# A GELU feed-forward kernel on one Trainium2 core: two opening loads move from SyncE's DMA queue to ScalarE's

## The chip, the cores and the metric

The kernel runs on one core of one Trainium2 chip. The metric is device time in microseconds (us), the median of several runs. One more execution was taken with the hardware profiler; all rows below are from that one. Its times are counted from the first instruction.

## What is computed

Two dense layers with a tanh-approximated GELU between them, all tensors in bf16:

```python
B, S, D, F = 1, 2048, 448, 1792
# x: (B, S, D)   w1: (D, F)   b1: (F)   w2: (F, D)   b2: (D)
h = einsum("bsd,df->bsf", x, w1) + b1
h = gelu(h, approximate=True)
out = einsum("bsf,fd->bsd", h, w2) + b2
```

## The kernel before

**Tiling.** The 2048 rows of x are cut into four chunks of 512 (`SC`), the 1792 hidden columns into 14 tiles of 128 (`ft`). D = 448 isn't a multiple of 128, so it is held in four slots whose first rows are `KROW = [0, 128, 256, 320]`; slots 2 and 3 overlap by 64 rows, and each hidden tile is summed from three full slots and one half (lines 229 and 237). The first layer writes PSUM with the hidden column on the partitions, ScalarE applies GELU with b1 as its bias and writes `g_sb` (L340), the second layer multiplies `g_sb` with w2 (L317), and VectorE adds b2 (L358). SyncE stores the result.

**Order.** `schedule` runs seven blocks of eight hidden tiles and the second layer's chunks between them, in an order written out by hand. There is no planner: each engine has its own program, and semaphores join them.

**The opening.** x for chunk 0 is loaded in rows, not transposed, into `xn_sb` (four row groups of 128 rows each, 512 rows in all). It comes in two halves of 224 KB: groups 0 and 1 on `sem_xn[0]` (L172), groups 2 and 3 on `sem_xn[1]` (L173). TensorE transposes it by matmuls with an identity (L214), in the six parts of `XPARTS`; VectorE and ScalarE copy the parts in turn from PSUM to `xT_sb` (L352 and L336). The first two parts need the first half of x, the third and all later ones the second half too. Ahead of the third part stands a small matmul that turns b1 (L205).

`opening_block` (L247) then runs block 0, eight hidden tiles with one PSUM bank each, slot by slot:

- slot 0 of w1 for the eight tiles. Its columns 0 to 1023 come in two pieces of 512 columns, 128 KB each (`W0_PIECES`, L146): tile 0 waits for piece 0 on `sem_w10[0]`, tile 4 for piece 1 on `sem_w10[1]`. Tile 0 also waits until VectorE has copied the first slot's two parts (`sem_xTd` at 2, L257); the other tiles wait for the copies that free their banks;
- slot 1 for the eight tiles, behind `sem_w1[1]` (L265);
- slots 2 and 3, behind `sem_w1[2]` and `sem_w1[3]` (L268, L269), then the halves.

Block 1 begins behind `sem_w1r` (L312), the remaining columns of w1. From there on no load is near: w2 is first used when the second layer's chunk 0 runs.

**The loads.** SyncE issues, in this order: the two halves of x (L172, L173), the two pieces of w1's slot 0 (L146), slots 1, 2 and 3 up to column 1024 (L150, 256 KB each), the rest of w1 (L151, L154), the transposing loads of x's chunk 1 (L164), w2 (L158), b2 (L178) and the transposing loads of chunks 2 and 3. ScalarE issues b1 (L330, 3.5 KB), then loads its activation table and runs a throwaway activation (L332), then copies its three parts of x (L336). The profile names SyncE's queue of data packets q1 and ScalarE's q10.

```python
sp.dma_start(xn_sb[:, 0:2, :], x0_view[:, 0:2, :]).then_inc(sem_xn[0], 16)
sp.dma_start(xn_sb[:, 2:4, :], x0_view[:, 2:4, :]).then_inc(sem_xn[1], 16)
load_w1(sp)
load_xT(sp, 1)
```

Of the kernel before, what the change touches and what calls it, by code (L numbers as in the profile page):

```python
# [11 lines left out]
def bass_standalone__dense_activation_gelu__prompt_kernel(  # L12
# [10 lines left out]
    P = 128  # L23
# [15 lines left out]
    W0_PIECES = [(0, 4), (4, 8)]  # L39
# [45 lines left out]
    for what, c in schedule:  # L85
        if what == "l1":
            jobs += [("g", order.index(tile)) for part in BLOCKS[c] for tile in part]
        else:
            jobs += [("o", n) for n, (j, _, _) in enumerate(outs) if j // STC == c]
    number = {job: n for n, job in enumerate(jobs)}  # L90

    with ExitStack() as es:
        sb = lambda n, s, d: es.enter_context(nc.sbuf_tensor(n, s, d))
        xT_sb = sb("xT_sb", [P, NKT, S], BF16)
        w1_sb = sb("wi_sb", [P, NKT, F], BF16)
        w2_sb = sb("wo_sb", [P, NFT, D], BF16)
        xn_sb = sb("xn_sb", [P, STC, D], BF16)
# [10 lines left out]
        sem_w10 = [S_(f"sem_w10_{i}") for i in range(len(W0_PIECES))]  # L108
# [4 lines left out]
        sem_xn = [S_(f"sem_xn{i}") for i in range(2)]  # L113
# [17 lines left out]
        x0_view = x2[0:SC, :].rearrange("(p t) d -> p t d", t=STC)  # L131
        out0_view = out2[0:SC, :].rearrange("(p t) d -> p t d", t=STC)

        def out_dram(j):
            return out0_view[:, j, :] if j < STC else out2[j * P:(j + 1) * P, :]

        def x_part(n, parts):
            h, k = parts[0]
            to = xT_sb[:, k:k + len(parts), 2 * h * P:2 * (h + 1) * P]
            src = ps[XBANK + n][:, 0:2 * P * len(parts)]  # L140
            return to, src.rearrange("p (k t) -> p k t", k=len(parts))

        def load_w1(eng):
            with nc.allow_non_contiguous_dma(reason="w1 column pieces"):
                for i, (a, b) in enumerate(W0_PIECES):
                    eng.dma_start(  # L146
                        w1_sb[:, 0, a * P:b * P], w1[0:P, a * P:b * P]
                    ).then_inc(sem_w10[i], 16)
                for k, r in list(enumerate(KROW))[1:]:
                    eng.dma_start(w1_sb[:, k, 0:WCUT], w1[r:r + P, 0:WCUT]).then_inc(sem_w1[k], 16)  # L150
                eng.dma_start(  # L151
                    w1_sb[:, 0:3, WCUT:F], w1[0:3 * P, WCUT:F].rearrange("(k p) f -> p k f", p=P)
                ).then_inc(sem_w1r, 16)
                eng.dma_start(w1_sb[:, 3, WCUT:F], w1[KROW[3]:D, WCUT:F]).then_inc(sem_w1r, 16)  # L154

        def load_w2(eng, i):
            a, b = W2_PIECES[i]
            eng.dma_start(  # L158
                w2_sb[:, a:b, :], w2[a * P:b * P, :].rearrange("(ft p) d -> p ft d", p=P)
            ).then_inc(sem_w2[i], 16)  # L160

        def load_xT(eng, c):
            for k, d0 in enumerate(KROW):
                eng.dma_start(  # L164
                    xT_sb[:, k, c * SC:(c + 1) * SC],
                    x2[c * SC:(c + 1) * SC, d0:d0 + P],
                    transpose=True,
                ).then_inc(sem_x[c], 16)

        @block.sync  # L170
        def _(sp):
            sp.dma_start(xn_sb[:, 0:2, :], x0_view[:, 0:2, :]).then_inc(sem_xn[0], 16)  # L172
            sp.dma_start(xn_sb[:, 2:4, :], x0_view[:, 2:4, :]).then_inc(sem_xn[1], 16)  # L173
            load_w1(sp)
            load_xT(sp, 1)
            for i in range(len(W2_PIECES)):
                load_w2(sp, i)
            sp.dma_start(b2_bc[:, :], b2.partition_broadcast(P)).then_inc(sem_b2, 16)  # L178
            for c in range(2, NSC):
                load_xT(sp, c)  # L180
            for j in range(NST - 1):
                sp.wait_ge(sem_osb, j + 1)
                sp.dma_start(out_dram(j), out_sb[:, j, :]).then_inc(sem_od, 16)
            sp.wait_ge(sem_od, 16 * NST)
# [11 lines left out]
        def _(pe):  # L196
# [5 lines left out]
            for n, (_, parts) in enumerate(XPARTS):  # L202
                if n == 2:
                    pe.wait_ge(sem_b1n, 16)
                    pe.matmul(  # L205
                        ps[NB - 1][:, 0:NFT], lhsT=b1n_sb[:, :], rhs=ident[0:NFT, 0:NFT],
                        start=True, stop=True,
                    ).then_inc(sem_b1T, 1)
                for h, k in parts:
                    if (h, k) in ((0, 0), (1, 0)):  # L210
                        pe.wait_ge(sem_xn[h], 16)
                    for t in range(2):
                        col = parts.index((h, k)) * 2 * P + t * P
                        mm = pe.matmul(  # L214
                            ps[XBANK + n][:, col:col + P],
                            lhsT=xn_sb[:, 2 * h + t, KROW[k]:KROW[k] + P],
                            rhs=ident[:, :],
                            start=True, stop=True,
                        )
                mm.then_inc(sem_xtp, 1)  # L220
# [25 lines left out]

            def opening_block(first, second):  # L247
                first = [ft for _, ft in first]
                second = [ft for _, ft in second]

# [77 lines left out]
        @block.scalar  # L328
        def _(act):
            act.dma_start(b1n_sb[:, :], b1.rearrange("(c p) -> c p", p=P)).then_inc(sem_b1n, 16)  # L330
            zero = nc.const_aps.tensor(0.0, [P, 8], FP32)
            act.activation(act_junk[:, :], zero, ACT.Gelu_apprx_tanh)  # L332
            for n, (e, parts) in enumerate(XPARTS):
                if e == "a":
                    act.wait_ge(sem_xtp, n + 1)
                    act.copy(*x_part(n, parts)).then_inc(sem_xTa, 1)  # L336
            act.wait_ge(sem_b1, 1)
            for i, (c, ft) in enumerate(order):
                act.wait_ge(sem_l1, i + 1)
                act.activation(  # L340
                    g_sb[:, ft, c * SC:(c + 1) * SC], bank("g", i)[:, :], ACT.Gelu_apprx_tanh,
                    bias=b1_f[:, ft:ft + 1], scale=1.0,
                ).then_inc(sem_g, 1)
            act.wait_ge(sem_osb, len(outs))
            act.dma_start(out_dram(NST - 1), out_sb[:, NST - 1, :]).then_inc(sem_od, 16)
# [44 lines left out]
```

## Time and profile before

| | us |
|---|---|
| median of 3 runs (lowest to highest) | 96.71 (96.46 to 96.75) |
| the profiled execution | 96.25 |
| its span, from the first to the last instruction | 94.4 |
| around the span in that execution | 1.85 |
| TensorE matmuls busy (granted clock 1.0 throughout) | 90.5 |
| ScalarE busy | 35.9 |
| VectorE busy | 11.7 |
| data moved, mean over the span | 7.50 MB, 79 GB/s |

A row of the timeline gives the start and the length in us, the engine, the line, the operation, what it writes and reads, how many instructions the row merges, and in brackets the idle time before it with what ended it. PE is TensorE's matmul side, PEld its weight loads, SPq and ACTq the sequencers of SyncE and ScalarE as they issue DMAs. The length of an issue isn't that of its transfer: from the start of an issue to the last of the sixteen semaphore increments of its transfer (its landing) it took

| load, line | issue starts | issue to landing | lands |
|---|---|---|---|
| x, first half, L172 | 0.74 | 2.5 | 3.2 |
| x, second half, L173 | 1.19 | 2.7 | 3.9 |
| w1 slot 0, piece 0, L146 | 1.65 | 3.5 | 5.1 |
| w1 slot 0, piece 1, L146 | 2.12 | 3.4 | 5.5 |
| w1 slot 1, L150 | 2.60 | 4.6 | 7.2 |
| w1 slot 2, L150 | 3.07 | 4.8 | 7.9 |
| w1 slot 3, L150 | 3.55 | 5.0 | 8.6 |

### The profile page before, as it was taken

How to read it: one execution, taken by the hardware profiler on the slowest of the kernel's cores; microseconds unless marked ns; L12 is line 12 of the kernel's file. 1: busy time of each engine (PE TensorE's matmuls, PEld its weight loads, DVE VectorE, ACT ScalarE, POOL GpSimd, SP SyncE). 2: the span in 40 equal slices, each digit the busy share in tenths (PEclk: the TensorE clock that was granted, in tenths of full speed). 3: DMA queues.
4: the chain of work that ended last, by engine and by line, in shares of the span. 5: the costliest groups of instructions: out<-in, count | busy, mean ns of one | idle time of the engine just before them, and what ended most of it. 6: DMA issues, size and time to landing. Idle time of an engine off the chain costs nothing.

```text
span 94.4 us, 1159 instructions
## 1 busy us (share of the span) xinstructions
PE 90.5 (96%) x492; PEld 43.8 (46%) x492; DVE 11.7 (12%) x21; ACT 35.9 (38%) x61; POOL 0.7 (1%) x6
## 2 busy tenths in 40 slices
PE   6989999999999999999999999999999999999990
PEld 4724343443443555544344455554345555555670
DVE  0320000000000022220000001222000222222130
ACT  3520595985958910000793990000099000000000
POOL 2000000000000000000000000000000000000000
PEclk9999999999999999999999999999999999999999
DMA  1999999998520010011000001110000110011111
GB/s 36 275 312 280 192 225 350 301 74 166 111 56 0 0 49 28 27 49 49 3 0 0 0 0 49 49 53 24 28 0 0 49 48 16 33 49 56 49 49 49
DMA packets 12385, 7.50 MB, mean 79 GB/s; under 512 B 7004, under 2 KB 11996, under 8 KB 12380
## 3 DMA queue, kind: packets, MB, share of 16 engines
q1 hardware_dynamic: 12208, 7.31, 32.9%
q10 hardware_dynamic: 172, 0.12, 0.4%
q8 instruction: 4, 0.07, 0.3%
q14 instruction: 1, 0.01, 0.0%
HBM read 4.02 MB, written 1.84 MB: 62 GB/s over the span
## 4 chain that ended last, share of the span: by engine, by line
PE 90%; DMA 5%; SPq 2%; DVE 0%; issue 0%
PE ps L317 45%; PE ps L229 38%; PE ps L237 7%; DMA wi_sb<-in_w_dram 5%; SPq L146 1%; SPq L173 0%; SPq L172 0%; DVE out_sb L358 0%
## 5 line engine op out<-in xcount | busy, mean ns | idle before, releaser
L340 ACT ACTIVATE g_sb<-ps,bi_f 128x512 bf16<-128x512 f32 x56 | 33.1, 702 | 34.9 <-PE ps L237 34.9
L317 PE MATMUL ps<-wo_sb,g_sb 128*128 128x448 bf16 (+2 forms) x238 | 42.9, 341 | 0.0
L229 PE MATMUL ps<-xT_sb,wi_sb 128*128 128x512 bf16 x168 | 38.2, 380 | 0.6 <-DMA wi_sb<-in_w_dram 0.4
L317 PEld LDWEIGHTS ps<-wo_sb,g_sb 128*128 128x128 bf16 x238 | 23.1, 98 | 19.7
L229 PEld LDWEIGHTS ps<-xT_sb,wi_sb 128*128 128x128 bf16 x168 | 15.7, 98 | 21.8 <-issue 3.0
L358 DVE TENSOR_TENSOR out_sb<-ps,bo_bc 128x448 bf16<-128x448 f32 (+2 forms) x17 | 10.2, 597 | 76.8 <-PE ps L317 76.8
L237 PE MATMUL ps<-xT_sb,wi_sb 64*128 64x512 bf16 x56 | 7.3, 379 | 0.0
L237 PEld LDWEIGHTS ps<-xT_sb,wi_sb 64*128 64x128 bf16 x56 | 2.2, 94 | 4.6 <-issue 3.0
L200 PE MATMUL ps<-const-bfloat16-1.0 128*128 128x256 bf16 x13 | 2.9, 410 | 0.8 <-PEq L375 0.8
L200 PEld LDWEIGHTS ps<-const-bfloat16-1.0 128*128 128x128 bf16 x13 | 1.8, 140 | 1.5 <-issue 0.7
L352 DVE CAST xT_sb<-ps 128x256 bf16<-128x256 f32 (+1 forms) x3 | 1.4, 510 | 3.8 <-PE ps L214 3.8
L332 ACT ACT_TABLE_LOAD x1 | 1.3, 1283 | 1.4 <-PEq L375 1.4
L336 ACT CAST xT_sb<-ps 128x256 bf16<-128x256 f32 (+1 forms) x3 | 1.3, 443 | 1.1 <-PE ps L214 1.0
L214 PE MATMUL ps<-ident,xn_sb 128*128 128x128 bf16 x16 | 1.2, 220 | 0.0
L214 PEld LDWEIGHTS ps<-ident,xn_sb 128*128 128x128 bf16 x16 | 1.0, 98 | 0.2
L190 POOL TENSOR_SCALAR_AFFINE_SELECT ident<-ident 128x128 bf16<-128x128 bf16 x1 | 0.3, 292 | 0.2 <-POOL ident L188 0.2
L332 ACT ACTIVATE act_junk<-const-float32-0.0 128x8 bf16<-128x8 f32 x1 | 0.2, 208 | 0.0
L188 POOL MEMSET ident<- 128x128 bf16 x1 | 0.2, 204 | 0.3 <-POOLq L375 0.3
L205 PE MATMUL ps<-ident,bin_sb 14*128 14x14 bf16 x1 | 0.2, 177 | 0.0
L354 DVE COPY bi_f<-ps 128x14 f32<-128x14 f32 x1 | 0.2, 161 | 0.0
L205 PEld LDWEIGHTS ps<-ident,bin_sb 14*128 14x128 bf16 x1 | 0.1, 90 | 0.1
L375 POOL MEMSET const-bfloat16-1.0<- 128x1 bf16 x1 | 0.1, 102 | 0.0
(3 smaller groups left out, 0.3 us busy)
## 6 DMA issues: line engine op xcount, KB each, us to landing
out_dram<-out_sb SPq DMA_DIRECT2D x15, 112.0 KB, 1.7
wo_sb<-in_w_dram SPq DMA_DIRECT2D x2, 784.0 KB, 6.5
wi_sb<-in_w_dram SPq DMA_DIRECT2D x3, 256.0 KB, 4.8
wi_sb<-in_w_dram SPq DMA_DIRECT2D x1, 576.0 KB, 6.8
xn_sb<-in_x_dram SPq DMA_DIRECT2D x2, 224.0 KB, 2.6
wi_sb<-in_w_dram SPq DMA_DIRECT2D x2, 128.0 KB, 3.4
wi_sb<-in_w_dram SPq DMA_DIRECT2D x1, 192.0 KB, 6.9
xT_sb<-in_x_dram SPq DMA_TRANSPOSE x12, 5.0
```

The source lines that it names most:

```text
L146: eng.dma_start(w1_sb[:, 0, a * P:b * P], w1[0:P, a * P:b * P]).then_inc(sem_w10[i], 16)
L200: pe.matmul(ps[0][:, 0:WN], lhsT=ones_w, rhs=ones_x, start=True, stop=True)
L205: pe.matmul(ps[NB - 1][:, 0:NFT], lhsT=b1n_sb[:, :], rhs=ident[0:NFT, 0:NFT], start=True, stop=True,).then_inc(sem_b1T, 1)
L214: mm = pe.matmul(ps[XBANK + n][:, col:col + P], lhsT=xn_sb[:, 2 * h + t, KROW[k]:KROW[k] + P], rhs=ident[:, :], start=True, stop=True,)
L229: return pe.matmul(bank("g", order.index((c, ft)))[:, :], lhsT=w1_sb[:, k, ft * P:(ft + 1) * P], rhs=xT_sb[:, k, c * SC:(c + 1) * SC], sta ...
L237: return pe.matmul(bank("g", order.index((c, ft)))[:, :], lhsT=w1_sb[lo:lo + HALF, k, ft * P:(ft + 1) * P], rhs=xT_sb[lo:lo + HALF, k, c * ...
L317: mm = pe.matmul(bank("o", n)[:, 0:c1 - c0], lhsT=g_sb[:, ft, j * P:(j + 1) * P], rhs=w2_sb[:, ft, c0:c1], start=(ft == 0), stop=(ft == NF ...
L332: act.activation(act_junk[:, :], zero, ACT.Gelu_apprx_tanh)
L336: act.copy(*x_part(n, parts)).then_inc(sem_xTa, 1)
L340: act.activation(g_sb[:, ft, c * SC:(c + 1) * SC], bank("g", i)[:, :], ACT.Gelu_apprx_tanh, bias=b1_f[:, ft:ft + 1], scale=1.0,).then_inc( ...
L352: dve.tensor_copy(*x_part(n, parts)).then_inc(sem_xTd, 1)
L358: dve.tensor_tensor(out=out_sb[:, j, c0:c1], in0=bank("o", n)[:, 0:c1 - c0], in1=b2_bc[:, c0:c1], op=ALU.add,).then_inc(sem_osb, 1)
```

## The change

ScalarE issues the second half of x and piece 1 of w1's slot 0, in this order, directly behind b1 and ahead of its activation table. SyncE issues the first half of x, then piece 0, then slots 1 to 3 and all the rest in the order of before. No wait, buffer, semaphore or computation changes. `load_w1_piece(eng, i)` is the loop body of `load_w1` as a function of its own.

```diff
+        def load_w1_piece(eng, i):
+            a, b = W0_PIECES[i]
+            with nc.allow_non_contiguous_dma(reason="w1 column pieces"):
+                eng.dma_start(
+                    w1_sb[:, 0, a * P:b * P], w1[0:P, a * P:b * P]
+                ).then_inc(sem_w10[i], 16)
+
         def load_w1(eng):
             with nc.allow_non_contiguous_dma(reason="w1 column pieces"):
-                for i, (a, b) in enumerate(W0_PIECES):
-                    eng.dma_start(
-                        w1_sb[:, 0, a * P:b * P], w1[0:P, a * P:b * P]
-                    ).then_inc(sem_w10[i], 16)
                 for k, r in list(enumerate(KROW))[1:]:
...
         def _(sp):
             sp.dma_start(xn_sb[:, 0:2, :], x0_view[:, 0:2, :]).then_inc(sem_xn[0], 16)
-            sp.dma_start(xn_sb[:, 2:4, :], x0_view[:, 2:4, :]).then_inc(sem_xn[1], 16)
+            load_w1_piece(sp, 0)
             load_w1(sp)
...
         def _(act):
             act.dma_start(b1n_sb[:, :], b1.rearrange("(c p) -> c p", p=P)).then_inc(sem_b1n, 16)
+            act.dma_start(xn_sb[:, 2:4, :], x0_view[:, 2:4, :]).then_inc(sem_xn[1], 16)
+            load_w1_piece(act, 1)
             zero = nc.const_aps.tensor(0.0, [P, 8], FP32)
```

## The prediction, made before the changed kernel was run

> **What bounds the kernel now.** TensorE's matmuls are busy for 90.5 of 94.4 us. I read the chain of waits first (its shares by line, then its pieces), then the timeline of the first 12 us, then the DMA's rates.
>
> ```profile
> PE ps L317 45%; PE ps L229 38%; PE ps L237 7%; DMA wi_sb<-in_w_dram 5%; SPq L146 1%; SPq L173 0%; SPq L172 0%; DVE out_sb L358 0%
> ```
>
> TensorE is the bound, and the only transfer in the chain is a load of w1. In order of time:
>
> ```profile
> 2.60 4.58 DMA wi_sb<-in_w_dram
> 7.18 0.05 issue
> 7.22 2.76 PE ps L229 x12
> 9.99 0.97 PE ps L237 x8
> ```
>
> From 7.22 us the chain stays on TensorE until VectorE's last add at 91.91. So the change's worth is read at one place: by how much does TensorE's start on w1's slot 1, now 7.22, move? What follows shifts with it one for one, unless a later load comes too late. Such waits stand behind slot 3 (lands 8.6; slot 1's eight matmuls last until 7.22 + 8 x 0.22 = 8.98, so 0.4 spare) and the rest of w1 (the later of its two issues starts at 4.50 and lands 6.9 later, 11.4; block 1 needs it at 9.99 + 0.97 + 4 x 0.22 = 11.84, 0.4 spare). 0.22 is one matmul of 512 columns: 24 of them take 5.29 us where the chain runs at 16.78.
>
> ```profile
> 0.74 0.39 SPq L172 DMA_DIRECT2D xn_sb<-in_x_dram  x1
> ...
> 0.75 0.65 ACTq L330 DMA_DIRECT2D bin_sb<-in_b_dram  x1
> ...
> 1.19 0.42 SPq L173 DMA_DIRECT2D xn_sb<-in_x_dram  x1
> 1.43 1.28 ACT L332 ACT_TABLE_LOAD   x1 [1.43 <-PEq L375]
> 1.65 0.91 SPq L146 DMA_DIRECT2D wi_sb<-in_w_dram  x2
> 2.60 1.38 SPq L150 DMA_DIRECT2D wi_sb<-in_w_dram  x3
> 2.72 0.21 ACT L332 ACTIVATE act_junk<-const-float32-0.0 128x8 bf16<-128x8 f32 x1
> ...
> 3.91 1.48 ACT L336 CAST xT_sb<-ps 128x256 bf16<-128x256 f32 x3 [0.98 <-PE ps L214]
> ...
> 5.17 4.81 PE L229 MATMUL ps<-xT_sb,wi_sb 128*128 128x512 bf16 x20 [0.40 <-DMA wi_sb<-in_w_dram]
> ```
>
> TensorE starts slot 0 at 5.17, released by piece 0 (1.65 + 3.5). Slot 0 then lasts 8 x 0.22 = 1.76, until 6.93, and 0.29 us go by until slot 1 lands. x itself was ready sooner: its second half lands at 3.88, VectorE's second copy ends 4.25 + 0.42 = 4.67, and 0.05 later tile 0 could have begun, at 4.72. I use **x's second half plus 0.84** for that below.
>
> Is it the issuing or the moving that makes slot 1 late? The table by stretches answers (the last two columns are the share of the 16 DMA engines that was busy, in us, and GB/s):
>
> ```profile
> 2.00:3.00 1.00, 1.00 (x6) 0.73 (x5) 0.00 (x0) 0.92 (x2) 0.00 (x0) 1.00 0.87 287
> 3.00:4.00 1.00, 1.00 (x11) 0.63 (x10) 0.20 (x1) 0.09 (x1) 0.00 (x0) 1.00 0.92 253
> 4.00:5.00 1.00, 0.77 (x12) 0.60 (x12) 0.97 (x3) 0.85 (x3) 0.00 (x0) 1.00 0.82 249
> 5.00:6.00 1.00, 0.83 (x4) 0.41 (x5) 0.35 (x2) 0.39 (x1) 0.00 (x0) 1.00 0.97 340
> 6.00:7.00 1.00, 1.00 (x5) 0.29 (x3) 0.00 (x0) 0.00 (x0) 0.00 (x0) 1.00 0.93 294
> ```
>
> From 2 us on the engines are 82 to 97% busy: mostly the moving. Ahead of slot 1's last byte stand 2 x 229 KB of x, 2 x 131 KB of slot 0 and its own 262 KB (in thousands of bytes), 982 in all, and the change takes none away.
>
> **The change, part by part.** *SyncE loses two issues*, 0.42 + 0.43 and their gaps: its issue of slot 1 starts at 1.65 instead of 2.60, 0.95 sooner, and so do those behind it, transposing loads and w2 included. Those are covered: chunk 1's x lands at 13.4 and is first used in the second part of block 1, past 16. Slot 1's gain is between 0.95 (were the issuing the limit) and 0 (were it the moving). By the busy shares I take 0: a request that stands longer in a full queue.
>
> *ScalarE gains two issues* ahead of its table. b1's ends at 0.75 + 0.65 = 1.40; one issue costs between 0.38 (ScalarE's own store at the end, 92.30) and 0.65 (b1). So x's second half is issued at 1.44 instead of 1.19, and the table, 1.43 now, starts between 2.30 and 2.84. Table and throwaway activation (1.28 + 0.21 and small gaps) end between 3.8 and 4.35; the first copy stands at 3.91 and is late by 0 to 0.44. That copy is slot 1's part of x, used after 7; the banks that these copies free are wanted from 5.6 on. Cost 0; with the cover gone 0.44.
>
> *The order in the DMA engines changes*, and this is the part with a price. Do two queues share an engine finely? b1, on ScalarE's queue, shows it beside x's first half. From 1.7 to 2.5 us:
>
> ```profile
> q1 hardware_dynamic: 73, 0.13, 72.0%
> q10 hardware_dynamic: 26, 0.00, 2.7%
> ```
>
> x's half is 128 packets and 16 increments, b1 14 and 14. Of b1 26 of 28 had gone by when x had some 73 of 144: ScalarE's packets got in between SyncE's, not behind them. So I take one packet of each queue in turn. [...]
>
> Packet by packet, x's second half (8 per engine) now shares its time with piece 0 (8 per engine), where it had the engines to itself. *It lands* between 4.13 (3.88 plus the 0.25 of later issue, no sharing) and 5.13 (both end together, where piece 0 lands now). I take the middle, 4.63. Tile 0 then starts at 4.63 + 0.84 = 5.47, 0.30 later, between 5.13 (by piece 0) and 5.97. Slot 0 would end at 5.47 + 1.76 = 7.23: alone this costs 0.01, as the 0.29 of waiting for slot 1 swallow it; at 5.97 it would cost 0.51.
>
> *Piece 1* had been ahead of slot 1; now the two share, 8 packets against 8, and end together. Slot 1's sixteen increments in the trace's semaphore record: fifteen by 6.20, the last, of one slow engine, at 7.18. Piece 1 lands between the two (from 5.48 of now, were it not to share); middle 6.69. Tile 4 wants it at 5.47 + 0.88 = 6.35. So TensorE stalls, resumes at 6.74, and four tiles of slot 0 end at 6.74 + 0.88 = 7.62: **0.40 later than 7.22**. At 7.18, 7.23 + 0.88 = 8.11, 0.89 later. The two delays don't add: the later one decides. Slots 2, 3 and the rest of w1 follow on SyncE's queue behind the same bytes as before, and TensorE comes later to them.
>
> **Sum:** 96.25 + 0.40 = 96.65 for an execution like the profiled one. The median of the runs lies 0.46 above it, so 96.71 + 0.40 = **97.1 us**.
>
> **Rivals.**
>
> *A, forecast: piece 1 and x's second half come late.* +0.1 to +0.9, so 96.8 to 97.6. For it: b1's interleaving, busy engines. Against: slot 1's 7.18 is one engine's; without that engine's lag piece 1 lands near 6.2, and nothing is lost. Chance 0.64, of which 0.06 lie within the bound of no change.
>
> *B, nothing moves:* engines serve the loads in nearly the old order, or the 0.29 of waiting swallow all. 96.7. Against: only a narrow set of landings does it (piece 1 between 6.0 and 6.6). Chance 0.08.
>
> *C, faster: the issuing was the limit.* The engines have 8 to 18% of idle time from 2 to 5 us, in which a second queue could feed them, and the 1 KB rows of slot 0 run at 249 to 253 GB/s where slot 1 runs at 340. If slot 1 comes 0.95 sooner (6.23) and x's second half stays at 3.88, tile 0 starts at 4.72 and slot 0 ends at 6.48: 0.74 won, 95.97. If x slips to 4.13 and piece 1 holds, tile 0 starts at 4.97, slot 0 ends at 6.73: 0.49 won, 96.22. It decides from the point where piece 1 lands before tile 4 wants it and slot 1 before 6.9. Against: x's second half must keep its landing beside piece 0's packets. Chance 0.28, 0.03 of it within the bound.
>
> **How the numbers follow.** About 0.3%, 0.29 us, is what a measurement of this kernel can tell from no change. Faster: 0.28 - 0.03 = 0.25. Same: 0.08 + 0.06 + 0.03 = 0.17. Slower: 0.64 - 0.06 = 0.58. The time is A's middle, 97.1. The range reaches from C's 96.2 to A's upper end with a little for the runs' scatter, 97.7; A's own is 96.8 to 97.6.
>
> **What would show it.** x's second half landing after 4.1 and tile 0 starting after 5.17: the sharing is real. An idle stretch of TensorE in the middle of slot 0's eight matmuls, ended by a load of w1: piece 1 is late. Slot 1's landing near 7.2 in spite of an issue at 1.65: the moving is the limit; at 6.3 it was the issuing, and I am wrong. A table load ending before 4.35 with tile 0 unaffected: ScalarE's issues are free.

## The result, and the profile after

| | before | after |
|---|---|---|
| median of 15 runs each, us (lowest to highest) | 96.46 (96.06 to 96.78) | 97.11 (96.87 to 98.61) |
| profiled execution / its span, us | 96.25 / 94.4 | 97.07 / 95.2 |

The ratio is 1.0072, 95% interval 1.0051 to 1.0092: the change makes the kernel slower by 0.65 us (median against median), between 0.5 and 0.9 by the interval. Ratios, here and below, leave out the few executions that ran slow throughout (the 98.61 is one); the medians are of all.

The chain of waits after (start, length, what):

```profile
1.42 0.36 ACTq L334
1.78 0.03 issue
1.81 5.34 DMA wi_sb<-in_w_dram
7.15 0.05 issue
7.20 3.41 PE ps L232 x15
10.61 0.15 issue
10.76 1.04 PE ps L240 x8
```

Before, the transfer in the chain was slot 1, issued by SyncE at 2.60, and TensorE came out of the wait at 7.22 with all of slot 0 done. Now it is piece 1 of slot 0, issued by ScalarE at 1.81, and TensorE comes out at 7.20 with four of slot 0's eight matmuls still ahead of it. The halves begin at 10.76 where they began at 9.99. (Of lines before, 214, 229 and 237 are now 217, 232 and 240; in some kernels below they are one more.) The timeline after:

```profile
1.19 0.41 SPq L146 DMA_DIRECT2D wi_sb<-in_w_dram  x1
1.42 0.36 ACTq L334 DMA_DIRECT2D xn_sb<-in_x_dram  x1
1.65 1.38 SPq L153 DMA_DIRECT2D wi_sb<-in_w_dram  x3
1.81 0.44 ACTq L146 DMA_DIRECT2D wi_sb<-in_w_dram  x1
2.29 1.28 ACT L337 ACT_TABLE_LOAD   x1 [2.29 <-issue]
...
4.54 1.46 PE L217 MATMUL ps<-ident,xn_sb 128*128 128x128 bf16 x12 [0.29 <-DMA xn_sb<-in_x_dram]
...
5.79 4.82 PE L232 MATMUL ps<-xT_sb,wi_sb 128*128 128x512 bf16 x19
...
7.20 3.14 PEld L232 LDWEIGHTS ps<-xT_sb,wi_sb 128*128 128x128 bf16 x16 [0.64 <-DMA wi_sb<-in_w_dram]
```

Three times matter here. x's second half is there for the transposes at 4.54 (before: 3.93). Tile 0 starts at 5.79 (5.17). The weights of tile 4 go in at 7.20, after a wait that a load of w1 ended. From the trace's semaphore records, the landings (all sixteen increments in):

| load | before | after | the changed kernel again (e11) |
|---|---|---|---|
| x, second half | 3.88 | 4.49 | 4.34 |
| w1 slot 0, piece 0 | 5.13 | 3.93 | 3.78 |
| w1 slot 0, piece 1 | 5.48 | 7.15 | 6.85 |
| w1 slot 1 | 7.18 | 6.59 | 6.68 |
| w1 slot 3 | 8.58 | 8.01 | 8.09 |

Piece 0 and the slots gained, x's half lost 0.6 and piece 1 lost 1.7. Slot 0's four last matmuls end at 7.20 + 4 x 0.22 = 8.08, 0.86 after the 7.22 at which slot 1 began before. The two spans differ by 0.8. Not all of the 0.86 is piece 1's: tile 0 started 0.62 late, and without the stall, which began at 6.89, slot 0 would have ended at 6.89 + 0.88 = 7.77, 0.55 late. How much is whose is what the experiments ask.

### The profile page after: what moved, and what is told of

Same layout as the page of the kernel before. It is cut to its first block, busy times and chain, and to the rows that moved or that the text cites. A ratio compares the mean times of both kernels' runs of the same rounds, so it can differ in the third digit from the quotient of the medians.

```text
span 95.2 us, 1153 instructions
## 1 busy us (share of the span) xinstructions
PE 90.9 (95%) x486; PEld 44.6 (47%) x492; DVE 11.8 (12%) x21; ACT 35.9 (38%) x61; POOL 0.7 (1%) x6
## 3 DMA queue, kind: packets, MB, share of 16 engines
q1 hardware_dynamic: 11920, 6.95, 30.2%
## 4 chain that ended last, share of the span: by engine, by line
PE 89%; DMA 6%; ACTq 1%; issue 1%; ACT 1%; DVE 0%
PE ps L320 45%; PE ps L232 37%; PE ps L240 7%; DMA wi_sb<-in_w_dram 6%; ACT g_sb L345 1%; ACTq L333 1%; ACTq L334 0%; DVE out_sb L363 0%
## 5 line engine op out<-in xcount | busy, mean ns | idle before, releaser
L232 PE MATMUL ps<-xT_sb,wi_sb 128*128 128x512 bf16 x162 | 37.2, 381 | 0.6 <-issue 0.2
L217 PE MATMUL ps<-ident,xn_sb 128*128 128x128 bf16 x16 | 2.1, 312 | 0.3 <-DMA xn_sb<-in_x_dram 0.3
L217 PEld LDWEIGHTS ps<-ident,xn_sb 128*128 128x128 bf16 x16 | 1.7, 142 | 0.6 <-DMA xn_sb<-in_x_dram 0.4
```

Of the source, the lines that this page charges most:

```text
L217: mm = pe.matmul(ps[XBANK + n][:, col:col + P], lhsT=xn_sb[:, 2 * h + t, KROW[k]:KROW[k] + P], rhs=ident[:, :], start=True, stop=True,)
L232: return pe.matmul(bank("g", order.index((c, ft)))[:, :], lhsT=w1_sb[:, k, ft * P:(ft + 1) * P], rhs=xT_sb[:, k, c * SC:(c + 1) * SC], sta ...
```

## The experiments

Theories that the expectations name, guesses until a run decided: S and P are about the order in which the DMA engines serve the two queues (whole shares in turn; packet by packet), X and T about the cost (X: x's late half and the slow transposes behind it; T: piece 1's late turn). Each kernel ran beside the kernel before, whose median lay between 96.40 and 96.48 us. e5 ran four times, the others twelve.

| run | ratio to before (95%) | median, us |
|---|---|---|
| e1, x's half alone | 1.0001 (0.9981 to 1.0021) | 96.38 |
| e2, piece 1 alone | 1.0019 (1.0002 to 1.0035) | 96.55 |
| e3, slot 1 held back | 1.0033 (1.0005 to 1.0060) | 96.84 |
| e4, changed + 3 warm-ups | 1.0045 (1.0022 to 1.0068) | 96.88 |
| e5, ScalarE's two swapped | 1.0484 (1.0446 to 1.0522) | 101.31 |
| e6, e1 + 3 warm-ups | 1.0025 (1.0003 to 1.0046) | 96.67 |
| e7, before + 3 warm-ups | 1.0005 (0.9985 to 1.0025) | 96.60 |
| e8, x's half first, then b1 | 1.0005 (0.9981 to 1.0030) | 96.43 |
| e9, x's half, b1, piece 1 | 1.0026 (1.0006 to 1.0045) | 96.71 |
| e10, x's half, piece 1; b1 on SyncE | 0.9986 (0.9962 to 1.0011) | 96.38 |
| e11, the changed kernel again | 1.0045 (1.0016 to 1.0074) | 97.04 |
| e12, changed, piece 1 used later | 1.0010 (0.9988 to 1.0033) | 96.68 |

**One of the two loads alone.** First x's second half:

```diff
 # against the changed kernel
             load_w1_piece(sp, 0)
+            load_w1_piece(sp, 1)
             load_w1(sp)
...
             act.dma_start(xn_sb[:, 2:4, :], x0_view[:, 2:4, :]).then_inc(sem_xn[1], 16)
-            load_w1_piece(act, 1)
```

> Three theories stand. S: a DMA engine serves a load's whole share from one queue before it turns to the other, so piece 1 stood behind slot 1 (it landed at 7.15, slot 1 at 6.59) and TensorE lost its time in the stall ahead of tile 4, from 6.89 to 7.20 and then four tiles more. P: the queues share packet by packet, and piece 1 and slot 1 end together; the stall is the same. X: what costs is the second half of x, late by 0.61, with the half-speed transposes that followed it. This kernel moves the second half of x alone; piece 1 goes back to SyncE, ahead of slot 1. S and P: piece 1 lands by 5.6, tile 4 doesn't wait, slot 1 lands near 7.2; the time is 0 to +0.3 us against the kernel before. X: tile 0 still starts near 5.8 and most of the loss stays, +0.5 to +0.7.

Measured: no change, 1.0001. The chain of this kernel:

```profile
1.43 3.05 DMA xn_sb<-in_x_dram
4.48 0.05 issue
4.52 1.16 PE ps L218 x12
5.68 4.32 PE ps L233 x20
10.00 0.97 PE ps L241 x8
```

x's half lands as late as in the changed kernel (4.48 against 4.49), and now it is what the chain waits for. But twenty matmuls (slots 0 and 1, and four of slots 2 and 3) follow without a gap and the halves begin at 10.00, where they began at 9.99 before: the 0.3 us that TensorE used to wait for slot 1 pay for it. Piece 1 landed at 5.19. X falls as the whole cause.

Then piece 1 alone:

```diff
 # against the changed kernel
+            sp.dma_start(xn_sb[:, 2:4, :], x0_view[:, 2:4, :]).then_inc(sem_xn[1], 16)
             load_w1_piece(sp, 0)
...
-            act.dma_start(xn_sb[:, 2:4, :], x0_view[:, 2:4, :]).then_inc(sem_xn[1], 16)
             load_w1_piece(act, 1)
```

> Piece 1 alone moves to ScalarE, behind b1; both halves of x stay with SyncE, ahead of piece 0. S: piece 1 is ready at about 2.6 and gets its turn after one of SyncE's loads ahead of slot 1, so it lands by 5.2; piece 0 may lose a turn to it and land up to 0.35 later. Time -0.1 to +0.3 against the kernel before. P: piece 1 shares with the second half of x and with piece 0, lands by 5.2 as well. X: the second half of x lands at 3.9 to 4.2, so nothing is lost, -0.1 to +0.2. If the move of piece 1 to the other queue is bad in itself, whatever stands ahead of it, +0.4 or more.

Measured: +0.18 us by the ratio, within what was expected. Piece 1, issued at 1.42, landed at 4.49, ahead of piece 0 (issued at 1.65, landed at 5.21). In this run it isn't slow on ScalarE's queue; in the changed kernel it stood behind x's half there, was issued at 1.81, and slot 1 had been issued at 1.65.

**Slot 1 held back, and more warm-up.** Two edits of the changed kernel:

```diff
 # e3
             load_w1_piece(sp, 0)
+            sp.wait_ge(sem_xn[0], 16)
             load_w1(sp)
 # e4
-    NWARM = 13
+    NWARM = 16
```

> The changed kernel, but SyncE waits for the landing of x's first half (3.28) before it issues slot 1, so no packet of slot 1 stands beside piece 1. S: piece 1 follows the second half of x directly and lands by 5.2 instead of 7.15; slot 1 is issued at 3.3 and lands at 7.0 to 7.5; tile 4 doesn't wait; against the kernel before 0 to +0.5, so faster than the changed kernel by 0.2 to 0.7. X: tile 0 starts near 5.8 as in the changed kernel, slot 0 ends at 7.5: +0.3 to +0.6.

> The changed kernel with 16 warm-up matmuls instead of 13, so that TensorE has work until about 4.1, and x's second half finds it at full speed more often. X: tile 0 starts at about 5.4 instead of 5.79 and the time falls by 0.3 to 0.5 against the changed kernel. S and P: tile 0 starts sooner, but tile 4 still waits for piece 1 at 7.1; no change against the changed kernel (within 0.15), +0.5 to +0.8 against the kernel before.

Held back (issued at 3.43 instead of 1.65), slot 1 let piece 1 through: it landed at 4.84 and tile 4 didn't wait. The cost fell to +0.33% from the changed kernel's +0.72%, and their intervals just overlap. Most of what was left is X's part: tile 0 started at 5.76, with its transposes at half speed (12 in 1.46 us, against 0.84 before), and the halves at 10.38. But the edit has a price of its own. It holds back every later load too: the rest of w1 landed at 12.23 (before: 11.40), and block 1 waited for it, which put 0.12 us between two matmuls there. In e4 the transposes ran at full speed (12 in 0.84 us), but its x half happened to land at 5.10 and piece 1 at 6.95; +0.45%, not to be told from the changed kernel. Neither run settles the share of the slow transposes.

**The order in the engines.** ScalarE's two loads the other way round, against the changed kernel:

```diff
-            act.dma_start(xn_sb[:, 2:4, :], x0_view[:, 2:4, :]).then_inc(sem_xn[1], 16)
             load_w1_piece(act, 1)
+            act.dma_start(xn_sb[:, 2:4, :], x0_view[:, 2:4, :]).then_inc(sem_xn[1], 16)
```

> The changed kernel with ScalarE's two loads in the other order: b1, piece 1, then the second half of x. S (whole shares in turn): piece 1 takes the place that x's half had, after piece 0, and lands by 4.6; x's half goes behind slot 1 and lands at 6.3 to 7.2, slot 1 before it by 0.4 or more in most of the engines. Tile 0 then starts at 7.1 to 8.4 and slot 1 at 8.9 to 10.2: +1.7 to +3.0 us against the kernel before. P (packet by packet): x's half and slot 1 end together, the sixteen increments of both in the same stretch; piece 1 and piece 0 end together too.

Measured: +4.8%, 4.7 us, more than S's 1.7 to 3.0. x's half, now the one behind slot 1's issue, landed at 7.52 against slot 1's 7.35, and the lag was 0.2 us from the first increments on (5.48 against 5.30): by P's sign they shared packet by packet. Piece 1, behind piece 0, landed at 4.34 against 3.93. So in this run S holds for the one pair and P for the other. The trace's packet records carry the queue, not the engine. But many packets start just 4 or 3 ns before the end of another (in the changed kernel's first 9 us 1399 and 819 pairs, against 304 to 534 at any other distance from -15 to 19 ns). Taking those as successions on one engine, one can count what follows what, less the matches that chance gives (seen at other distances). Each load has 128 packets and 16 increments, taken as 8 packets for each of 16 engines:

```
what follows what, counts         changed kernel   e5 (swapped)
x's half   -> x's half                  97               2
x's half   -> a slot of w1               0             109
a slot     -> x's half                  -1             128
piece 0    -> piece 0                  120             104
piece 0    -> ScalarE's next load       -1               4
piece 1    -> piece 1                   45             101
piece 1    -> a slot of w1              62               0
a slot     -> piece 1                   74               1
```

In the changed kernel x's half ran whole (97), behind piece 0; piece 1 alternated with the packets of the slots of w1 (62 and 74). In e5 it is x's half that alternates (109 and 128). In these two profiles the load of ScalarE that is issued after slot 1 (piece 1 at 1.81 in the one, x's half at 1.82 in the other) is the one that shares with the slots. The queues' rows in the changed kernel, from 4.3 to 6.7 us, show piece 1 going its way beside the slots:

```profile
q1 hardware_dynamic: 277, 0.51, 73.9%
q10 hardware_dynamic: 142, 0.13, 17.2%
```

The rest of e5's cost is TensorE's speed:

```profile
7.57 1.46 PE L217 MATMUL ps<-ident,xn_sb 128*128 128x128 bf16 x12 [3.30 <-DMA xn_sb<-in_x_dram]
...
8.82 1.49 PE L232 MATMUL ps<-xT_sb,wi_sb 128*128 128x512 bf16 x3
```

After 3.30 us of idling the twelve transposes take 1.46 instead of the 0.84 of before, as they did after 0.29 in the changed kernel, and the twenty matmuls of the slots, 4.32 in e1's chain, take 6.19 here: 0.6 and 1.9 us that the expectation had left out. The trace's record of the granted clock, whose first entry, at full speed, begins at 3.47 us in the profile before and at 6.26 in the changed kernel's, begins here at 12.70 only; up to there the matmuls of 512 columns start 0.43 us apart, from there on 0.22.

**More warm-up without the late piece 1.** e6 is e1, e7 the kernel before, each with `NWARM = 16` in place of 13.

> The kernel that moves x's second half alone, with 16 warm-up matmuls instead of 13. There TensorE's start on tile 0 hangs on x's half and the transposes behind it (from 4.52 on, some at half speed), no longer on piece 0. If the half speed costs there, the transposes fall from 1.16 to 0.84 us and the time by 0.1 to 0.3 against the kernel before, so that this beats both kernels. If slot 1's landing is the bound anyway: within 0.1 of the kernel before.

> Control for the one ahead of it: the kernel before with 16 warm-up matmuls instead of 13, no load moved. The first half of x is transposed 0.6 later, from 4.1, which piece 0's landing at 5.1 hides; where the runs of the kernel before met the half-speed clock this takes it away. Expected -0.1 to +0.1 us. If it gains as much as the one ahead of it, the gain is the warm-up's and not the queue's.

e6 missed: it got slower by 0.25%, not faster. Its transposes did run in 0.84 us, but in its profile the last of the sixteen increments of x's half came at 5.08 (fifteen were in by 4.34), so tile 0 started at 6.02. e7 changed nothing (1.0005). Neither run shows a gain from the warm-up.

**x's half first, and the two theories apart.** In e8 and e9 ScalarE issues x's half before b1; in e8 piece 1 is SyncE's, in e9 it is issued by ScalarE behind b1. In e10 ScalarE issues x's half and piece 1, and b1 goes to SyncE.

```diff
 # e9, ScalarE (e8: without its last line, and SyncE issues piece 1 behind piece 0)
+            act.dma_start(xn_sb[:, 2:4, :], x0_view[:, 2:4, :]).then_inc(sem_xn[1], 16)
             act.dma_start(b1n_sb[:, :], b1.rearrange("(c p) -> c p", p=P)).then_inc(sem_b1n, 16)
-            act.dma_start(xn_sb[:, 2:4, :], x0_view[:, 2:4, :]).then_inc(sem_xn[1], 16)
             load_w1_piece(act, 1)
 # e10, ScalarE without b1; SyncE
             sp.dma_start(xn_sb[:, 0:2, :], x0_view[:, 0:2, :]).then_inc(sem_xn[0], 16)
+            sp.dma_start(b1n_sb[:, :], b1.rearrange("(c p) -> c p", p=P)).then_inc(sem_b1n, 16)
             load_w1_piece(sp, 0)
```

> ScalarE issues the second half of x first, at 0.75, then b1; SyncE issues the first half, pieces 0 and 1, slot 1 and the rest. By S the halves of x follow each other as before and piece 0 comes after them: x's second half lands at 3.8 to 4.0, piece 0 at 4.5 to 5.1, slot 1 near 6.2 to 7.2. The issuing is 0.47 sooner for all of SyncE's loads of w1. If the moving is the limit, within 0.15 of the kernel before; if the issuing had a share in it, -0.2 to -0.4. b1 lands about 0.5 later, at 3.4, ahead of x's second half; no cost.

> ScalarE issues x's second half first, then b1, then piece 1; SyncE as in the changed kernel. So x's half comes at 3.9 to 4.1, as where it was issued first with piece 1 left to SyncE (that cost nothing), and only piece 1, issued at about 1.9 behind slot 1's issue at 1.65, is late. Theory T, piece 1's late turn is the cause: it lands at 6.4 to 7.2, tile 4 waits for it, +0.4 to +0.9 us against the kernel before. Theory X, x's late half with the half-speed transposes behind it is the cause: x comes in time, so -0.1 to +0.2.

> The same two loads on ScalarE, but first there: x's half at 0.75, piece 1 at about 1.15, half a microsecond or more before SyncE issues slot 1 (about 2.3); b1 goes to SyncE behind x's first half. T: piece 1 gets its turns before slot 1 has packets at the engines and lands by 5.3, tile 4 doesn't wait: -0.1 to +0.2 against the kernel before. If loads on ScalarE's queue are slow in themselves: +0.4 or more.

e8: nothing, 1.0005, though SyncE issued slot 1 0.48 sooner. The time alone doesn't say that the moving is the limit, as TensorE didn't wait for slot 1 here: tile 0 started at 5.34, slot 0 lasted until 5.34 + 1.76 = 7.10, and slot 1 was in at 6.75. The landings say more. Fifteen of slot 1's sixteen increments were in by 6.63 in e8 and by 6.02 in e1, which issues it as early, against 6.20 before: no steady gain from the sooner issue. e9: piece 1, issued at 1.89 behind slot 1's 1.65, landed at 7.00 in the profile, and TensorE shows the same stall, with x's half in by 4.21 (and the first half, issued at 0.74 against its 0.75, by 4.03, where it was in by 3.23 before; tile 0 started at 5.61):

```profile
5.61 1.02 PE L232 MATMUL ps<-xT_sb,wi_sb 128*128 128x512 bf16 x4
7.04 3.13 PEld L232 LDWEIGHTS ps<-xT_sb,wi_sb 128*128 128x128 bf16 x16 [0.91 <-DMA wi_sb<-in_w_dram]
7.04 3.41 PE L232 MATMUL ps<-xT_sb,wi_sb 128*128 128x512 bf16 x15 [0.41 <-DMA wi_sb<-in_w_dram]
```

Over its twelve runs it cost 0.26%, 0.25 us by the ratio: less than T's 0.4 to 0.9, and between the two theories. e10: both loads on ScalarE and no loss, 0.9986. Piece 1, issued at 1.18, landed at 4.47. With e2, where piece 1 is ahead as well (issued at 1.42 against 2.13), this says that in these runs not the queue decides but whether piece 1 is issued ahead of slot 1.

**The changed kernel again, and piece 1 used later.** e12 leaves the loads as changed and lets TensorE run slot 1 for tiles 0 to 3 before slot 0 for tiles 4 to 7:

```diff
                     full(0, ft, 0, True, False)
-                pe.wait_ge(sem_w1[1], 16)
-                for n, ft in enumerate(fts):
+                    if n == 3:
+                        pe.wait_ge(sem_xTa, 2)
+                        pe.wait_ge(sem_w1[1], 16)
+                        for early in fts[:4]:
+                            full(0, early, 1, False, False)
+                for n, ft in enumerate(fts[4:]):
                     full(0, ft, 1, False, False)
```

> The changed kernel once more, beside the runs of the one that uses piece 1 later. If its loss is as first measured: +0.5 to +0.9 us against the kernel before. If chips or hours differ: less, like the +0.25 of the kernel in which piece 1 alone was late.

> The loads as in the changed kernel; TensorE runs slot 1 for tiles 0 to 3 before slot 0 for tiles 4 to 7, so that it wants piece 1 about 0.88 us later, and slot 1 as soon as four matmuls are done. T (piece 1's lateness is what costs): the stall ahead of tile 4 goes, slot 1 for tiles 0 to 3 runs from about 6.6 to 6.9 on, and piece 1 at 7.2 is there in time; -0.3 to -0.6 us against the changed kernel. X (x's late half and the half-speed transposes): tile 0 starts at 5.3 to 5.8 as before, no gain beyond 0.1 against the changed kernel.

e11's profile is the cleanest view of the cause, as here x came early and the transposes ran at full speed:

```profile
4.38 0.84 PE L217 MATMUL ps<-ident,xn_sb 128*128 128x128 bf16 x12 [0.35 <-DMA xn_sb<-in_x_dram]
...
5.28 1.02 PE L232 MATMUL ps<-xT_sb,wi_sb 128*128 128x512 bf16 x4
...
6.89 0.33 PEld L232 LDWEIGHTS ps<-xT_sb,wi_sb 128*128 128x128 bf16 x3 [1.08 <-DMA wi_sb<-in_w_dram]
6.89 0.60 PE L232 MATMUL ps<-xT_sb,wi_sb 128*128 128x512 bf16 x2 [0.59 <-DMA wi_sb<-in_w_dram]
```

Tile 0 starts at 5.28, only 0.11 later than before; four matmuls; then 0.59 of nothing until piece 1. Slot 0 ends at 6.89 + 0.88 = 7.77, 0.55 late, and the span is 94.9 against 94.4. The stall alone makes this execution's loss: without it slot 0 would have ended at 5.28 + 1.76 = 7.04, ahead of the 7.22 of before. e12's profile has no stall:

```profile
4.50 1.33 PE ps L217 x12
5.83 4.32 PE ps L232 x20
10.15 0.97 PE ps L240 x8
```

Twenty matmuls without a gap, though tile 0 started later than in e11, at 5.67. This profile alone doesn't show that the order of use did it. In it piece 1 landed at 6.05, with the same loads as in e11: the engines moved 342 GB/s from 4.3 to 6.7 us, against 316 in e11 and 265 in the changed kernel's first profile. The changed kernel's order would have wanted piece 1 at 5.67 + 0.88 = 6.55 and not have stalled either. What shows it is the times. e12's ratio is 1.0010 where e11 beside it has 1.0045, and the medians are 0.36 us apart, in the expected 0.3 to 0.6. The two intervals overlap a little, but set directly against each other, the means of the executions that count for the ratios differ by 0.38 us (95% interval 0.1 to 0.7). Nothing here beats the kernel before: e8 and e10 equal it.

## Why the prediction was right, and where it wasn't

The direction, the place and the mechanism held: TensorE stalls ahead of tile 4, on piece 1, whose packets alternate with those of the slots of w1 (62 and 74 successions across) where it is issued behind slot 1 (at 1.81 against 1.65). Using piece 1 later takes most of the loss away (e12), issuing it ahead of slot 1, with x's half sooner too, all of it (e10). The prediction's words that the later of the two delays decides held too: in e11 the stall is the whole loss, while in the first profile tile 0's late start alone would have cost 0.55 of the 0.86. The time of 97.1 was met at 97.11, but partly by luck: the step forecast was +0.40 on a median of 96.71; measured was +0.65 on one of 96.46. By its steps:

- **SyncE's issues, 0.95 sooner, worth 0.** No run speaks against it: e1 and e8, with slot 1 issued 0.48 sooner, are no faster. Slot 1 did land sooner, at 6.59 instead of 7.18, between the two signs that the text had named (7.2 for the moving, 6.3 for the issuing). But 7.18 was one late increment: fifteen were in by 6.20 before and by 6.55 after. Which share the sooner issue had, and which that part of piece 1's bytes now stand behind slot 1, isn't told apart.
- **ScalarE's table and copies, cost 0.** Right. The table load starts at 2.29, the throwaway activation ends at 3.58 + 0.21 = 3.79, inside the cover, and the copy waited for the transposes.
- **x's second half at 4.63.** Measured 4.49 and 4.34, but not for the reason given. It didn't alternate with piece 0; it came whole behind it. The reading of b1's 26 packets, that the queues always turn packet by packet, was too general: b1 is 14 packets with 14 increments, one packet for each increment, so its row showed that ScalarE's packets got in between SyncE's there, not that the queues take turns. By the counts this pair went whole (97 of at most 112 successions stay inside x's half) and the other did not (45 inside piece 1 against 62 from piece 1 to a slot).
- **Tile 0 at 5.47.** Measured 5.79 and 5.28. The 0.84 from x's landing nearly held in e11 (4.34 to 5.28: 0.94) and not in the first profile (4.49 to 5.79: 1.30), where the transposes ran at half speed.
- **Piece 1 at 6.69, the middle of its bounds: the mis-sized term.** Measured 7.15 and 6.85, with the same loads in e4 and e12 6.95 and 6.05, and 7.00 in e9. Four of the five lie nearer the upper bound (7.18), which was one late increment of slot 1; the fifth lies below the lower one (6.20), so no single value holds. With 7.15 the same sum gives 7.20 + 0.88 - 7.22 = 0.86, the profiled execution's 0.8.
- **The 0.29 of waiting swallow x's delay.** Right: e1, ratio 1.0001.

**What stays open.** The sizes of the parts. Piece 1 late with x's half 0.3 us earlier costs 0.25 us (e9), x late with piece 1 in time 0.0 (e1) to 0.3 (e3, with its own price in it), both 0.4 (e11) to 0.7 (the first result). The intervals are too wide to say whether the parts add up. That two late arrivals, each different from run to run, make the later of them later still would fit, but it is only argued. Nor do the runs say why piece 0 and x's half kept whole where piece 1 and the slots alternated, or why in e12, with the same loads, piece 1 ran mostly whole: by the same count some 80 successions inside it and 26 to a slot.

## What to carry to other kernels

With the DMA engines 82 to 97% busy (before, from 2 to 7 us), moving loads to another queue bought nothing here (e1 1.0001, e8 1.0005, e10 0.9986) and in the changed kernel reordered the stream. Ask for each moved load what it is now issued behind, and which wait comes first in the program. What took the loss away here was to issue the load that is wanted first before the big ones of either queue (e10: piece 1 in by 4.47), or to let the consumer take the work whose data come first (e12: 1.0010 against e11's 1.0045). Piece 1 as ScalarE's second load stood behind the 0.36 us issue of x's half, from 1.42 to 1.81; slot 1 was issued at 1.65, so that was the difference between ahead of slot 1 and behind it.

## What the runs showed of the hardware

- In the changed kernel's profile the packets of the two queues followed each other in two manners within a few microseconds: whole loads in turn (piece 0, then x's half, its packets starting from 3.10 to 4.07: 97 successions inside it) and packet by packet (piece 1, from 4.21 to 6.66, and the slots: 62 and 74 successions across). In e8 x's two halves alternated (some 94 and 76 across by the same count).
- The last of a load's sixteen increments was late by itself in five of the fourteen profiled executions (before, e2, e4, e6, e10): one or two of the seven opening loads had it 0.7 to 1.0 us behind the fifteenth, and not the same loads. Before, slot 1's fifteenth was in by 6.20 and the last came at 7.18; in e6 fifteen of x's half were in by 4.34, the last came at 5.08, and the transposes that wait for all sixteen began at 5.12.
- Transposes ran 107 ns or 56 ns apart in kernels whose program ahead of them is the same (the changed kernel's two profiles: 12 in 1.46 and in 0.84 us), while the granted clock's column reads 1.00 in both. The column counts time without an entry in the trace's clock record as 1.00 (in e5, whose record begins at 12.70, it reads 1.00 from 7 to 11 us), and that record's first entry, at full speed, begins at 6.26 us in the one and at 3.56 in the other (6.30 in e2; 3.47 in the profile before, so the "throughout" of its table holds from there on). In e1 and e5 the spacing changes where it begins: in e1 at 5.22, between transposes 0.11 and 0.06 apart, in e5 at 12.70, from 0.43 to 0.22 between matmuls. So here the slow transposes go with the execution and not with the moved loads alone: e2, with x's half in by 4.09, has them too. Ahead of the first entry read the spacing, not the column.
